# A written order of all steps in place of one computed from ranks, in a DeltaNet and low-rank mixer kernel

## The chip, the cores and the metric

One NeuronCore of a Trainium2 chip runs the whole kernel. It has five engines with instruction streams of their own: TensorE (PE: matmuls, PEld: its weight loads), VectorE (DVE), ScalarE (ACT), GpSimd (POOL) and SyncE (SP, which here only issues DMAs). [...] The metric is the device time of one launch in microseconds; a lower time is better. A time is the median of several runs.

## The reference

A DeltaNet attention for 4 batches, 8 heads, 768 tokens and 48 channels, whose output `x` goes through a low-rank token mixer and a two-layer channel mixer:

```python
k_n = k / (np.linalg.norm(k, axis=-1, keepdims=True) + 1e-06)
for t in range(S):
    y[:, :, t] = np.einsum('bhd,bhde->bhe', q[:, :, t], state)
    v_old = np.einsum('bhde,bhd->bhe', state, kt)
    state = state + bt[:, :, :, None] * np.einsum('bhd,bhe->bhde', kt, vt - v_old)
x = y.transpose(0, 2, 1, 3).reshape(B, S, H * D)
h = x.transpose(0, 2, 1) @ U @ V
u = x + h.transpose(0, 2, 1)
return u + np.maximum(u @ w_ch1, 0.0) @ w_ch2
```

## The kernel before

**Work.** Tokens are cut into chunks of 64 (12 to a batch, `c`). Half a batch (6 chunks, all heads) is a unit `n`, eight in all; unit 2b and 2b+1 belong to batch `b`. Two large tiles, `slots`, hold the operands of an even and an odd unit, so that unit n+2 overwrites unit n. Of a unit the kernel makes, in this order:

- `load` (L531): DMAs of k, q, v and a second copy z of k, on SyncE's and GpSimd's queues, 4 heads each.
- `grams`: `turn` (L633) transposes k and q by TensorE, `placed` (L648) copies them out by ScalarE, `products` (L661) makes k k^T and k q^T, which ScalarE (L671, L681) and VectorE (L674, L692) copy and mask.
- `blocks` (L737 to L759): VectorE inverts the 32-row triangles by substitution, pairs of L746 and L752, between two transposes; `seed` (L731) clears the tile for it on GpSimd. `norms` (L593 to L610) scales it.
- `joins` (L768 to L869) and `diagonals` (L881, L888) put the triangles of 32 together to 64 by small matmuls (L802, L816, L842, L845, L860, L863).
- for units 0 and 1, `prepare` (L961, L972) multiplies the inverse into k and v ahead of the recurrence.

`recur(b)` then goes through the chunks of a batch: a product with the state (L1051 for units 0 and 1, L1010 and L1034 later), a subtraction (L1064 or L1022), the update's product (L1079) and the state's sum (L1089). `outputs` makes a chunk's y (L925, L939) and `put` copies it into the tile X (L909). Each of these products is 8 matmuls on quarters of TensorE's array.

The weights of the mixers come as 14 slices (`load_weights`): DMA (L1166), and per slice two VectorE steps (L1193, L1199), a ScalarE cast (L1174) and a third VectorE step (L1205) that frees the buffer for the slice after the next. `sums` (L1119) adds slices of the second matrix to one another.

The mixers work on blocks `i` of 256 tokens, three to a batch. `front` makes u and its transpose (L1372 to L1418). `wide` is the channel mixer: `channels` e = 0 to 5 multiplies by two column blocks of the first matrix, in a form of 128 rows (L1475, mode "F") or on quarters of 64 rows (`crossed`, L410, mode "Q", with a one-column copy L419 by ScalarE half way), `relu` (L1440) takes the result from PSUM, `add_up` (L1502) and `last_sum` form sums, `narrow` e = 0 to 3 does the seven products of the second matrix (L1590 or again L410), and `gather` (L1515) adds them into X and sends out a finished block. Batch 3's first layer is done by `quick` (L1275 and around), six strands of seven matmul steps each.

**PSUM.** Four pairs of banks take everything up to the mixers; when all but the last chunk of batch 0 is through, `reserve` takes the fourth pair away, and its two banks, the "mix" banks, belong to `channels`, `narrow` and `quick`.

**Order.** Each of the functions above is a generator. It yields either a list of keys that have to be emitted first (`need`) or a step `op(engine, cost, ...)`; resumed, it writes that step's instructions and goes on to its next yield. The order in which steps are resumed is the order in which instructions stand in the engines' streams; nothing reorders them afterwards, and the semaphores follow from which tiles a step reads and writes. `run` chooses the next step with a clock of its own for each engine: of the steps that can start soonest it takes the one with the lowest rank. The rank of a part is the number in the table `PLACES` under its name (`recur b0 -6.39`, some 600 entries), and an entry `quad 1` allows the part the 64-row form:

```python
at, i = min(picks)                       # earliest start, then lowest rank
cost = cost_of(s)                        # a written estimate of the step's time
state["now"] = clock[s["e"]] = at + cost
advance(i, got, state["now"] + s["lat"])
```

The order so found has 692 steps of TensorE, 720 of VectorE, 501 of ScalarE, 158 of GpSimd and 166 of SyncE.

Of the kernel before, what the change touches and what calls it, by code (L numbers as in the profile page):

```python
# [1 line left out]

# [5 lines left out]

# [8 lines left out]

# [6 lines left out]

QUADS = ((0, 0), (1, 1), (1, 0), (0, 1))


@with_exitstack
def kernel(
    ctx: ExitStack,  # L30
    tc: tile.TileContext,
    q: bass.AP,
    k: bass.AP,
    v: bass.AP,
    beta: bass.AP,
    moe_U: bass.AP,
    moe_V: bass.AP,
    moe_w_ch1: bass.AP,
    moe_w_ch2: bass.AP,
    out: bass.AP,  # L40
):

    nc = tc.nc  # L50

# [16 lines left out]
    W2 = 2 + 2 * KT  # L68

    const = ctx.enter_context(tc.tile_pool(name="const", bufs=1))  # L70
    single = ctx.enter_context(tc.tile_pool(name="single", bufs=1))
    small = ctx.enter_context(tc.tile_pool(name="small", bufs=2))
    conv = ctx.enter_context(tc.tile_pool(name="conv", bufs=2))
    mix = ctx.enter_context(tc.tile_pool(name="mix", bufs=2))
    scratch = ctx.enter_context(
        tc.tile_pool(name="scratch", bufs=2, space=bass.MemoryType.DRAM)
    )
    psum = ctx.enter_context(
        tc.tile_pool(name="psum", bufs=1, space=bass.MemoryType.PSUM)
    )  # L80

    P = psum.tile([128, 8, 512], FP32, name="P")
    BANK = dict(pair=[0, 2, 4, 6], mix=[6, 7])

    clock = dict(port=0.0, pe=0.8, dve=0.8, act=0.8, pool=0.8, sp=0.8)
    state = dict(now=0.0, mode=None, hw=0.0, slow=1.9, lot=69, fetched=0.0, flow=0.0, span=0)
    free = dict(pair={x: 0.0 for x in range(4)}, mix={})
    done, parts, waits, ready, last = {}, {}, {}, {}, {}  # L90
    asked, missing, awaited, woken, quads = {}, {}, {}, [], set()
    LAT = dict(pe=0.22, dve=0.06, act=0.06, pool=0.1, sp=0.0)
    SWITCH, HOLD, STAY = 0.18, 0.18, 0.15
    LOT, FETCH = 256, 4.1
    SPAN, PHASE = 3.413, 2.0

    def dve(n):
        return (n + 151) / 1000.0

    def act(n):  # L100
        return 0.16 + n / 1200.0

    def op(
        engine, cost, mode=None, take=None, give=(), lat=None, rush=None, words=0, port=None, flow=None,
        after=(),
    ):
        return dict(
            after=after,
            flow=cost * 0.95 if flow is None else flow,
            e=engine, cost=cost, mode=mode, take=take, give=give, words=words + 0.4,  # L110
            port=engine == "pool" if port is None else port,
            rush=bool(give) if rush is None else rush, lat=LAT[engine] if lat is None else lat,
        )
# [4 lines left out]
    def emitted(key, after=0.0):  # L118
        done[key] = state["now"] + after
        for i in awaited.pop(key, ()):  # L120
            missing[i].discard(key)
            if not missing[i]:
                woken.append(i)

    def landing(packets, each=0.0205):
        state["hw"] = max(state["hw"], state["now"] + 1.0) + packets * each / 16
        return state["hw"] + 0.4 - state["now"]

    def advance(i, value, at):
        try:  # L130
            s, ready[i] = parts[i].send(value), at
        except StopIteration:
            waits.pop(i, None)
            return
        if isinstance(s, list):
            waits.pop(i, None)
            asked[i], missing[i] = s, {key for key in s if key not in done}
            for key in missing[i]:
                awaited.setdefault(key, []).append(i)
            if not missing[i]:  # L140
                woken.append(i)
        else:
            waits[i] = s

    PLACES = """
    add_up b0 i0 17.5; add_up b0 i1 115.48; add_up b0 i2 71; add_up b1 i1 10.76; add_up b1 i2 15.15
    add_up b2 i0 54.56; add_up b2 i1 63.94; add_up b2 i2 115.5; add_up b3 i0 -4.22; add_up b3 i1 62.29
    add_up b3 i2 42; blocks n1 40.91; blocks n2 26.26; blocks n3 92.86; blocks n4 49.5; blocks n5 78.95
    blocks n6 36.67; blocks n7 136.31; both -6; channels b0 i0 e1 24.46; channels b0 i0 e2 52.34
    channels b0 i0 e3 47.17; channels b0 i0 e4 51.28; channels b0 i0 e5 -8.66; channels b0 i1 e0 52.04  # L150
    channels b0 i1 e0 quad 1; channels b0 i1 e1 79.42; channels b0 i1 e2 120.05; channels b0 i1 e3 96.5
    channels b0 i1 e3 quad 1; channels b0 i1 e4 13.79; channels b0 i1 e5 26.76; channels b0 i2 e0 quad 1
    channels b0 i2 e1 88.32; channels b0 i2 e1 quad 1; channels b0 i2 e2 92.17; channels b0 i2 e2 quad 1
    channels b0 i2 e3 128.97; channels b0 i2 e4 12; channels b0 i2 e4 quad 1; channels b0 i2 e5 88
    channels b0 i2 e5 quad 1; channels b1 i0 e0 40.95; channels b1 i0 e0 quad 1; channels b1 i0 e1 59
    channels b1 i0 e1 quad 1; channels b1 i0 e2 96.8; channels b1 i0 e2 quad 1; channels b1 i0 e4 91
    channels b1 i0 e4 quad 1; channels b1 i0 e5 69.5; channels b1 i0 e5 quad 1; channels b1 i1 e1 123.7
    channels b1 i1 e1 quad 1; channels b1 i1 e2 47.06; channels b1 i1 e2 quad 1; channels b1 i1 e3 -2.83
    channels b1 i1 e4 -16.29; channels b1 i1 e4 quad 1; channels b1 i1 e5 99.12; channels b1 i1 e5 quad 1
    channels b1 i2 e0 62.73; channels b1 i2 e0 quad 1; channels b1 i2 e2 35.08; channels b1 i2 e3 93.63  # L160
    channels b1 i2 e3 quad 1; channels b1 i2 e4 -29.18; channels b1 i2 e5 10.16; channels b1 i2 e5 quad 1
    channels b2 i0 e0 107; channels b2 i0 e1 41.61; channels b2 i0 e2 12.5; channels b2 i0 e2 quad 1
    channels b2 i0 e3 100.05; channels b2 i0 e3 quad 1; channels b2 i0 e4 17.5; channels b2 i0 e5 68.5
    channels b2 i1 e0 -1.5; channels b2 i1 e0 quad 1; channels b2 i1 e1 107.29; channels b2 i1 e1 quad 1
    channels b2 i1 e2 -7.68; channels b2 i1 e2 quad 1; channels b2 i1 e3 -3.95; channels b2 i1 e4 33.5
    channels b2 i1 e4 quad 1; channels b2 i2 e0 0.4; channels b2 i2 e0 quad 1; channels b2 i2 e1 22.31
    channels b2 i2 e1 quad 1; channels b2 i2 e2 21.63; channels b2 i2 e2 quad 1; channels b2 i2 e3 7.38
    channels b2 i2 e3 quad 1; channels b2 i2 e4 90.57; channels b2 i2 e5 quad 1; copies 0; cut 9
    diagonals n0 h0 -0.5; diagonals n0 h1 107.22; diagonals n1 h0 48.5; diagonals n1 h1 -9.5; diagonals n2 h0 12
    diagonals n2 h1 67.42; diagonals n4 h0 15; diagonals n4 h1 22.77; diagonals n5 h0 66.26; diagonals n5 h1 66.6  # L170
    diagonals n6 h0 49.61; diagonals n6 h1 75; diagonals n7 h0 65.5; diagonals n7 h1 71.44; first 71.59
    first_of_last 8.76; front b0 i0 46.95; front b0 i0 quad 1; front b0 i1 41.01; front b0 i2 58.06
    front b1 i0 30.2; front b1 i1 45.12; front b1 i2 142.26; front b1 i2 quad 1; front b2 i0 46.76
    front b2 i0 quad 1; front b2 i1 6.48; front b2 i1 quad 1; front b2 i2 66.34; front b3 i0 56.8
    front b3 i1 110.5; front b3 i2 18.13; gather b0 i0 h0 c1 70.62; gather b0 i0 h1 c0 116.5
    gather b0 i0 h1 c1 103.04; gather b0 i1 h0 c0 57.42; gather b0 i1 h0 c1 47.56; gather b0 i1 h1 c0 101.5
    gather b0 i1 h1 c1 114; gather b0 i2 h0 c0 78.4; gather b0 i2 h1 c0 54.71; gather b0 i2 h1 c1 59.36
    gather b1 i0 h0 c0 60.5; gather b1 i0 h0 c1 110; gather b1 i0 h1 c1 16.38; gather b1 i1 h0 c0 7
    gather b1 i1 h0 c1 0.46; gather b1 i2 h0 c0 81; gather b1 i2 h0 c1 76; gather b1 i2 h1 c0 93.52
    gather b1 i2 h1 c1 -12; gather b2 i0 h0 c0 67; gather b2 i0 h0 c1 29.97; gather b2 i0 h1 c0 26.5  # L180
    gather b2 i0 h1 c1 46.69; gather b2 i1 h0 c0 12.5; gather b2 i1 h0 c1 4; gather b2 i1 h1 c1 -0.93
# [76 lines left out]
    wide b0 i2 113.63; wide b1 i0 110.97; wide b1 i1 12; wide b1 i2 100.81; wide b2 i1 94; wide b2 i2 81.54  # L258
    wide b3 i1 10; wide b3 i2 -7.5
    """  # L260
    PLACES = dict(x.strip().rsplit(" ", 1) for x in PLACES.replace("\n", ";").split(";") if x.strip())

    def name_of(part):

# [42 lines left out]
    def late(s, at):  # L307

        over = state["lot"] + s["words"] - LOT
        if s["e"] != "pe" or over <= 0:  # L310
            return 0.0, 0.0
# [1357 lines left out]
```

## Time and profile before

| what | value |
|---|---|
| three runs | 611.9, 611.78, 609.16 us; median 611.78 |
| profiled execution, span | 609.6 us (its own time is not given apart from the span) |
| instructions in the profile | 24754 |
| costliest group | L1475, `channels` in 128-row form: 420 records, 97.2 us |
| second | L1590, `narrow`: 456 and 240 records, 79.5 and 41.6 us |
| third | L410, 64-row form: 912 records, 62.5 us |
| chain that ended last | PE 71%, DVE 8%, ACT 2%, issue 2% of the span |
| HBM | 27.03 MB read, 4.72 MB written |

A matmul in 32-bit floats leaves two records, so 12 records of L1475 are 6 matmuls. The span is the time from the first to the last instruction. A group of the profile is known by the source line that issued it and the tiles it writes and reads (`P<-ut,w_sb` writes PSUM from the transposed u and the first matrix). `<-ACT hs L1440` behind an idle time names what ended it; "issue" is idle time that ended without anything the profile shows. TensorE's granted clock is given as a share of its full speed.

### The profile page before, as it was taken

The numbers are of one execution on the slowest core, as the hardware profiler recorded it, in microseconds if no ns is written. First come the engines' busy times: TensorE is split into PE (matmuls) and PEld (weight loads), VectorE is DVE, ScalarE is ACT, GpSimd is POOL, SyncE is SP. The second block draws the span as 40 slices with busy tenths as digits, with TensorE's granted clock in tenths as the row PEclk, the third lists the DMA queues.
The fourth block names the chain that finished last, engine by engine and source line by source line (L and its number), as shares of the span: only waits on it lengthen the run. The fifth ranks groups of instructions, "written<-read, shape, count | busy, mean of one in ns | idle before, by whom it ended". The sixth has DMA issues, their size and how long they took to land.

```text
span 609.6 us, 24754 instructions
## 1 busy us (share of the span) xinstructions
PE 569.9 (93%) x11178; PEld 480.4 (79%) x11178; DVE 395.1 (65%) x972; ACT 235.9 (39%) x498; POOL 97.7 (16%) x169
## 2 busy tenths in 40 slices
PE   4797776999999998999999899999999999999997
PEld 4697765788889787888879767988888768656997
DVE  5889966798893232899899428998993225332542
ACT  3566863634242343344332633244225321344000
POOL 8321124420010126003005230020001000000000
PEclk9656575899999999999999999999999999999999
DMA  9951759610000156101006133020000000000000
GB/s 142 165 149 52 252 173 166 120 41 4 28 3 6 44 81 117 49 2 41 29 3 100 49 74 49 16 53 3 30 2 3 30 3 1 26 1 1 19 34 26
DMA packets 63849, 33.34 MB, mean 55 GB/s; under 512 B 50816, under 2 KB 61824, under 8 KB 63744
## 3 DMA queue, kind: packets, MB, share of 16 engines
q1 hardware_dynamic: 56800, 23.21, 17.7%
q0 software_dynamic: 5344, 8.27, 6.5%
q8 instruction: 87, 1.43, 1.0%
q10 hardware_dynamic: 1600, 0.30, 0.3%
q14 instruction: 18, 0.15, 0.1%
HBM read 27.03 MB, written 4.72 MB: 52 GB/s over the span
## 4 chain that ended last, share of the span: by engine, by line
PE 71%; DVE 8%; ACT 2%; issue 2%; DVEq 0%; ACTq 0%
PE P L1590 22%; PE P L1475 13%; PE P L410 12%; PE P L1275 7%; PE P L633 2%; PE P L661 2%; DVE xt L752 2%; DVE prod L746 2%; PE P L1034 2%; PE P L1010 1%; PE P L925 1%; PE P L1079 1%; ACT hs L1440 1%; PE P L1372 1%; PE P L939 1%
## 5 line engine op out<-in xcount | busy, mean ns | idle before, releaser
L1475 PE MATMUL P<-ut,w_sb 128*128 128x256 f32 x420 | 97.2, 384 | 0.2
L1475 PEld LDWEIGHTS P<-ut,w_sb 128*128 128x128 f32 x420 | 77.8, 190 | 11.2 <-ACT hs L1440 0.9
L1590 PE MATMUL P<-w_sb,hs 128*128 128x192 f32 x456 | 79.5, 329 | 0.0
L1590 PEld LDWEIGHTS P<-w_sb,hs 128*128 128x128 f32 x456 | 74.0, 190 | 2.8 <-ACT hs L1440 0.9
L1515 DVE TENSOR_TENSOR X<-X,P 128x192 f32<-128x192 f32 x85 | 29.6, 352 | 62.7 <-PE P L1590 55.1
L752 DVE TENSOR_TENSOR xt<-xt,prod 128x112 f32<-128x112 f32 (+21 forms) x200 | 64.6, 323 | 6.9
L746 DVE TENSOR_TENSOR prod<-gs,xt 128x112 f32<-128x112 f32 (+21 forms) x200 | 64.1, 321 | 4.9
L410 PE MATMUL P<-ut,w_sb 64*64 64x256 f32 x912 | 62.5, 384 | 1.2 <-ACT hs L1440 0.2
L1440 ACT ACTIVATE hs<-P 128x512 f32<-128x512 f32 x54 | 32.3, 597 | 74.0 <-PE P L1475 56.1
L531 POOL DMA_DIRECT2D slot<-in_k_dram x44 | 28.9, 664 | 95.4 <-PE P L1079 94.5
L1590 PE MATMUL P<-w_sb,S 128*128 128x192 f32 x240 | 41.6, 328 | 0.0
L633 PE MATMUL P<-ident,slot 128*128 128x128 f32 x192 | 31.6, 317 | 8.6 <-DMA slot<-in_k_dram 7.0
L909 ACT COPY X<-P 64x192 f32<-64x192 f32 x96 | 30.0, 312 | 24.0 <-PE P L939 22.0
L1590 PEld LDWEIGHTS P<-w_sb,S 128*128 128x128 f32 x240 | 39.0, 190 | 0.2
L410 PEld LDWEIGHTS P<-ut,w_sb 64*64 64x64 f32 x912 | 29.7, 133 | 10.5 <-ACT hs L1440 1.7
L648 ACT COPY slot<-P 128x768 f32<-128x768 f32 x30 | 23.5, 801 | 36.1 <-PE P L633 35.9
L1089 DVE TENSOR_TENSOR s<-s,P 128x192 f32<-128x192 f32 x40 | 14.0, 351 | 33.0 <-PE P L1079 30.2
L633 PEld LDWEIGHTS P<-ident,slot 128*128 128x128 f32 x192 | 25.8, 163 | 11.7 <-issue 9.7
L1275 PE MATMUL P<-slot,w_sb 128*128 128x384 f32 x96 | 34.6, 492 | 0.1
L881 ACT COPY slot<-zz 32x384 f32<-32x384 f32 x64 | 32.3, 509 | 6.1 <-DVE zz L759 4.7
L661 PEld LDWEIGHTS P<-slot 48*64 48x64 f32 x1536 | 29.3, 150 | 6.5 <-issue 2.8
L661 PE MATMUL P<-slot 48*64 48x64 f32 x1536 | 31.9, 237 | 0.6 <-ACT slot L648 0.5
(157 smaller groups left out, 966.1 us busy)
## 6 DMA issues: line engine op xcount, KB each, us to landing
out_dram<-X SPq DMA_DIRECT2D x22, 192.0 KB, 1.9
X<-in_moe_w_ch_dram SPq DMA_DIRECT2D x10, 384.0 KB, 4.2
wide<-in_moe_w_ch_dram SPq DMA_DIRECT2D x10, 384.0 KB, 4.5
slot<-in_k_dram SPq DMA_DIRECT2D x48, 72.0 KB, 5.0
slot<-in_k_dram POOLq DMA_DIRECT2D x44, 72.0 KB, 5.1
slot<-in_q_dram POOLq DMA_DIRECT2D x32, 72.0 KB, 5.0
slot<-in_q_dram SPq DMA_DIRECT2D x32, 72.0 KB, 5.0
slot<-in_v_dram POOLq DMA_DIRECT2D x32, 72.0 KB, 3.0
```

What stands on the lines that cost most here:

```text
L410: nc.tensor.matmul(to[half(g)], w[half(r), half(g)], x[half(r)], start=start, stop=stop, skip_group_check=True,)
L633: nc.tensor.transpose(p_t[:, c // 3, c % 3], t[:, c, 2 * j : 2 * j + 2].rearrange("p s d -> p (s d)"), ident,)
L661: nc.tensor.matmul(p_g[half(g ^ (par * i)), par, c], kq[rows, c, j, 0, half(g)], kq[rows, c, j, i, half(g)], start=True, stop=True,)
L746: nc.vector.tensor_tensor(out=prod, in0=gb[:, :, j : j + 1, j + 1 :].to_broadcast([128, split, m, w]), in1=xb[:, :, 0:m, j : j + 1].to_bro ...
L752: nc.vector.tensor_tensor(out=xb[:, :, 0:m, j + 1 :], in0=xb[:, :, 0:m, j + 1 :], in1=prod, op=ALU.subtract,)
L881: nc.scalar.copy(pg[quarter(i), :, at, :, a : a + BK], cut(zc, h)[quarter(i)].rearrange("p r (c j) t -> p r c j t", j=2),)
L909: nc.scalar.copy(x[half(c % 2), c // 2, 4 * D * g : 4 * D * (g + 1)].rearrange("p (j r d) -> p r j d", r=2, d=D), states(p_y)[half(g)],)
L1275: nc.tensor.matmul(to, w, t, start=start, stop=stop, skip_group_check=True)
L1440: nc.scalar.activation(hs[:, fs[0] : fs[1] + 1 : fs[1] - fs[0]], p_f, ACTF.Relu)
L1475: nc.tensor.matmul(p_f[:, x], w(x, t), ut[:, t], start=(t == 0), stop=(t == KT - 1))
L1515: nc.vector.tensor_tensor(out=to, in0=to, in1=p, op=ALU.add)
L1590: nc.tensor.matmul(to, of[0], of[1], start=of[2], stop=of[3], skip_group_check=True)
```

## The change

The planner goes: `PLACES`, the ranks, the engines' clocks, the costs in `op`, the bookkeeping of banks and the choice between the two forms. In its place stands a string `ORDER` of 2228 tokens. A token is the number of a part (parts are numbered as they begin); `38` resumes part 38, `14.0` resumes part 14 and gives it pair of banks 0, `269q` resumes part 269 in the 64-row form where both are offered. The order was found by exchanges of single steps.

```diff
-    def run():
-        stall, forms = {}, {}
-        while waits or woken:
...
+    ORDER = """
+    1 0 1 0 1 0 1 0 1 38 22 38 22 21 22 14.0 36 22 21 2 151 36 43 15.1 151 38 37 36 37 152 153.2 21 43 152 36
...
+    def run():
+        wake()
+        for token in ORDER.split():
+            i, bank, quad = (token.partition('q')[0] + '.').split('.')[0], token.partition('.')[2], 'q' in token
+            step = waits[int(i)]
+            if isinstance(step, tuple):
+                step = step[quad]
+            mode[0] = step['mode'] or mode[0]
+            fixed = step['take'][1] if isinstance(step['take'], tuple) else None
+            first = fixed[0] if isinstance(fixed, tuple) else fixed
+            advance(int(i), int(bank) if bank else first)
+            wake()
+        assert not waits and not awaited
```

Four waits that the clocks had implied are written into the generators' lists: a unit counts as read only when the outputs of its last three chunks are written; `relu` waits for weight slice 7, whose landing buffer is the tile it writes; a block of batch 3 waits for the sum of the block before. The last `channels` of a block is offered in the 128-row form alone:

```diff
             if cu == UC - 1:
-                emitted(("rec", n), 0.5)
+                yield [('y', b, c - 1), ('y', b, c - 2)]
+                emitted(('rec', n))
...
-        yield need(("front", b, i), ("half" if b == LAST else "narrow", *before(b, i), *[3] * (b == LAST)))
+        yield need(('front', b, i), *([('half', *before(b, i), 3), ('summed', *before(b, i), 6)] if b == LAST else [('narrow', *before(b, i))]))
...
         def relu(fs, ms, p_f):
-            yield op("act", act(2 * GT), give=[("mix", m) for m in ms])
+            yield [('weights', 7)]
+            yield op('act')
...
-            yield (
-                op("pe", 1.3, "F", take=("mix", y % 2), words=12),
-                op("pe", 0.87, "Q", take=("mix", (0, 1)), words=32),
-            )
-            if parted():
+            plain = op('pe', mode='F', take=('mix', y % 2))
+            last = y == len(PAIRS) - 1
+            yield (plain if last else (plain, op('pe', mode='Q', take=('mix', (0, 1)))))
+            if parted() and (not last):
```

The steps themselves, their tiles, buffers and queues are the same. The new order has 686 steps of TensorE (5658 matmuls for 5712: three `channels` with e = 5 change their form), 720 of VectorE, 498 of ScalarE, 158 of GpSimd and 166 of SyncE. Of TensorE's steps 389 stand in the same sequence as before, of VectorE's 408, of ScalarE's 268; a TensorE step that both orders have is moved by 4.9 places on average (at most 46), a VectorE step by 8.7 (at most 69).

## The prediction

> **What bounds the kernel now.** I read the page's busy times first, then the busy time by stage, then the chain of waits, and last the order of VectorE's instructions where the chain leaves TensorE.
>
> ```profile
> PE 569.9 (93%) x11178; PEld 480.4 (79%) x11178; DVE 395.1 (65%) x972; ACT 235.9 (39%) x498; POOL 97.7 (16%) x169
> ```
> ```profile
> PE   4797776999999998999999899999999999999997
> PEclk9656575899999999999999999999999999999999
> ```
> ```profile
> 0.00:111.00 111.00, 84.53 (x2436) 76.67 (x2440) 85.77 (x208) 64.01 (x121) 39.26 (x71) 0.65 0.74 158
> 111.00:606.00 495.00, 485.01 (x8758) 403.76 (x8746) 308.99 (x763) 171.86 (x378) 58.48 (x99) 1.00 0.15 32
> 606.00:610.00 4.00, 0.32 (x2) 0.02 (x1) 0.35 (x1) 0.00 (x0) 0.00 (x0) 0.83 0.08 25
> ```
>
> TensorE sets the end, in two unlike stages. In the second table each row is a stage: its length, then busy us of PE, PEld, DVE, ACT, POOL, then the granted clock. Up to 111 us (loads, the triangular solves, batch 0's recurrence) TensorE is idle for 111.0 - 84.5 = 26.5 us and runs at a mean clock of 0.65, VectorE being busy for 85.8 us: a chain through three engines bounds it. From 111 to 606 us TensorE is idle for 10 us and the clock is 1.00. The last 4 us are the final add and store.
>
> Busy time hides short waits, since a pipelined group that starts late still counts as busy. So I took each group of matmuls (one step of the order) from its start to the start of the next, and as its undisturbed time the 20th percentile of the same kind after 112 us. From 112 us to the end the groups take 42.8 us more than undisturbed, of some 498: that is what an order could at most give back there. 14.8 us of it stand at 102 changes of the matmul tiling (128, 64 or 32 rows), 0.145 us each. Four stretches of 1.29 to 1.72 us, 6.0 together, wait for nothing that the profile shows ("issue"). Most of the rest is short waits like these, on the chain of waits (start, us, what):
>
> ```profile
> 302.47 0.61 ACT hs L1440
> 303.12 1.09 PE P L410 x16
> 305.28 0.97 PE P L410 x16
> 307.28 0.60 ACT hs L1440
> 307.93 1.09 PE P L410 x16
> ```
>
> The chain leaves TensorE twice in 6 us for the 0.60 us activation that frees the two mix banks: only two groups of 0.41 us stand between the matmuls it reads and those that want the banks.
>
> **The change, part by part.** *The planner and its costs* run while the program is built: no instruction, 0 us. *The four added waits* are lists that hold a step back until other steps are written; no instruction, 0 us, whatever they forbid is already in the written order. *Three `channels` of e = 5* go from 64-row to 128-row form: 24 small matmuls become 6 large ones (54 fewer matmuls in all) and three L419 copies go (0.16 us each, on ScalarE, 39% busy). Both forms have the same array work: 6 records of L1475 take 1.29 us and 24 of L410 some 1.3 us, two of each to a channel; taken as 0, between -0.5 us (three copies that TensorE no longer waits for) and +0.9 us (six entries at 0.145). *Tiling changes* go from 129 to 131: 2 x 0.145 = +0.3 us.
>
> *The order after 112 us.* 337 groups of the old order there wait for a ScalarE or VectorE instruction. I call a cover short when the matmul time that stands between the group which that instruction waited for and the group which waits for it is less than the instruction's own time (with up to six queued ahead of it) plus 0.35 us of handing over; in the rows above an L1440 starts 0.25 us or so after its last matmul's group and the L410 behind it 0.05 us after its end, its weight load having waited 0.26. Old order: 54 short covers, new order: 25 of 329. In the trace a group with a short cover is late by 0.284 us on average (tiling changes left aside), another by 0.034. By number: 29 x 0.25 = 7.2 us gained. By name: 44 short covers go, with 9.7 us of lateness in the trace apart from tiling changes, less 1.7 of an "issue" stretch and 38 x 0.034 that stays: -6.7; 15 come, now 2.5 us late, 15 x 0.284 = 4.3 then: +1.8; net -4.9. I take -6.0, between the two. Example: for `channels` b1 i1 e1 of the rows above the new order puts the two halves of e0 side by side and three small groups (1.2 us) behind them.
>
> *VectorE beside it.* The substitutions of units 4 and 5 are drawn forward. Over 80 us of undisturbed matmul time from batch 0's second token block on, the new order holds 89.8 us of VectorE work; the old order's densest 80 us held 84.6, and the pace of the trace (498 for 455) gives such a stretch 87.5. Bounds: 0, if overlapping starts cover it as they do from 280 to 320 us (36.1 busy of 40), and +3.3, if VectorE decides and the gain there is lost with it. I take +1.5.
>
> *The start.* The recurrence of batch 0 stands on two waits for weight slices:
>
> ```profile
> 91.94 0.35 DVE L1064 TENSOR_TENSOR z<-slot,P 128x192 f32<-128x192 f32 x1 [1.22 <-PE P L1051]
> 94.17 0.56 DVE L1193 TENSOR_SCALAR power<-X 128x768 int32<-128x768 int32 x1 [1.87 <-DMA X<-in_moe_w_ch_dram]
> 94.64 0.74 DVE L1199 TENSOR_SCALAR X<-X 128x768 int32<-128x768 int32 x1
> 95.31 0.34 DVE L1089 TENSOR_TENSOR s<-s,P 128x192 f32<-128x192 f32 x1
> ...
> 99.72 0.56 DVE L1193 TENSOR_SCALAR power<-wide 128x768 int32<-128x768 int32 x1 [1.59 <-DMA wide<-in_moe_w_ch_dram]
> 100.20 0.35 DVE L1064 TENSOR_TENSOR z<-slot,P 128x192 f32<-128x192 f32 x1
> ```
>
> L1193 opens a weight slice. It waits 1.87 and 1.59 us for its DMA, and the recurrence's L1089 and L1064 are queued behind it, TensorE behind those (2.4 and 1.4 us). The new order writes the first of the two after the next chunk's update and the second two chunks later. The same 7.5 us of weight work stays among these chunks. Against that, slice 13 is asked for later too: its buffer is freed by a conversion that now comes two steps later, and on SyncE's queue the loads of unit 2 stand ahead of slices 12 and 13 (SP's issues take some 0.65 us each; this slice took 9.2 us from issue to use). So between 0 and 3.5 us are gained here. Earlier, batch 0's chunks 2 to 5 come forward by 5 to 8 us of matmul and VectorE work, but what unit 1's half needs (`prepare`, L961) has 4.0 us more of TensorE's and 3.5 us more of VectorE's work ahead of it, and four of its groups have covers short by 1.5 to 2 us behind ScalarE's queue: between 0 and +4. At `front` of batch 0 the work ahead is equal again on TensorE, VectorE and ScalarE. POOL's and SP's first loads are interleaved among each other with the same number of issues; 0. Start in all: I take -2.0, between -3.5 and +4.
>
> **Sum**: -6.0 + 1.5 - 2.0 + 0.3 = -6.2 us. The profiled execution has a span of 609.6; its own time is not shown, and the runs (609.2 to 611.9) put it within 2.3 us of the span. From the median: 611.8 - 6.2 = 605.6, say **605.5 us**.
>
> [...] The four "issue" stretches lie where small matmuls are dense (1.5 us before an L860), and the instruction queue moved 87 packets, 1.43 MB. [...]
>
> **The rivals.**
> 1. *More than that*: the start gives its whole 3.5 us and the "issue" stretches fall on other, slower groups (-4): 611.8 - 7.2 - 3.5 - 4 + 0.3 = 597. For it: they are few and depend on where a dense run meets a load. Against: the dense runs are still there. 0.13.
> 2. *VectorE becomes the bound* where units 4 and 5 are solved: the full 3.3 us, and of the 6.0 the third that lies there is lost: 611.8 - 4 + 3.3 - 1 = 610. For it: 84.6 to 89.8 us. Against: 65% over the span, and 5.8 us of work in the 20 us before. 0.13.
> 3. *Slower: unit 1 comes late.* If chunk 6 of batch 0 has to wait for `prepare` of unit 1, the start ends 4 us later by the queues ahead of it, and as TensorE has the full clock only from 110 us on, some 4 us of the mixer's first matmuls fall into half clock and cost 4 more: 611.8 + 8 - 4.5 = 615. It decides from the point at which `prepare` is later than the chunk before it, which in the old trace had some 4 us to spare (83.1 against 86.8 us). 0.13.
> 4. *The order does nothing*: the waits that go are replaced by the next one behind, as when a bank is held by two readers; 611 to 612. 0.09.
>
> [...]
>
> **How the numbers follow.** My forecast has 0.52. Range 597 to 613: it takes in rivals 1 and 2 and my own case (600 to 609), and leaves out most of rival 3. Within 0.5% (3 us) is no change that this measurement can tell: up to 608.7 is faster. Faster: 0.48 of my case, 0.13, 0.03 of rival 2: 0.64. Slower: 0.11 of rival 3 and a few hundredths: 0.14. Same: 0.22.
>
> **What would show it.** Right: from 112 us on fewer L1440 and L1089 on the chain, the rows "PE <- ACT hs L1440" and "PEld <- ACT hs L1440" smaller; between 111 and 606 us (or its counterpart) 4 to 6 us less; no DMA ahead of L1193's counterpart in batch 0's recurrence; the full clock from some 108 us. Wrong: DVE at 95% or more for 80 us with PE waiting for `rest` or `s`; the first `front` later than 111.5 us; "issue" stretches of more than 6 us.

## The result, and the profile after

The new order is slower: 620.1 us (median of 4 runs, 619.3 to 620.5) against 611.84 (4 runs, 609.2 to 613.4) beside it; the ratio is 1.013, 95% interval 1.0096 to 1.0164. The profiled execution after has a span of 617.6 us against 609.6, 8.0 us more.

Busy times, and TensorE with its clock in 40 slices, from the page of the kernel after:

```profile
PE 570.7 (92%) x11070; PEld 485.2 (79%) x11070; DVE 389.4 (63%) x972; ACT 232.2 (38%) x495; POOL 97.5 (16%) x169
```
```profile
PE   3768886899999999999999999999999999999997
PEclk9975655599999999999999999999999999999999
```

The stages of the kernel after, with the columns of the table in the prediction:

```profile
0.00:122.00 122.00, 88.36 (x2424) 81.20 (x2428) 85.12 (x208) 63.62 (x120) 37.17 (x68) 0.68 0.63 140
122.00:614.00 492.00, 482.00 (x8658) 404.00 (x8650) 303.88 (x763) 168.55 (x375) 60.31 (x102) 1.00 0.16 33
614.00:618.00 4.00, 0.30 (x2) 0.00 (x1) 0.35 (x1) 0.00 (x0) 0.00 (x0) 0.86 0.08 25
```

The busy times hardly moved, so work was not added; it stands at other times. The mixer's stage got shorter, 492 us where it took 495. The start got longer: TensorE is idle in it for 122.0 - 88.4 = 33.6 us, against 26.5. Measured at one point, the first group of the first `front` (batch 0), the start ends at 122.6 us in place of 111.5 (+11.2, with the decimals that the table leaves out), and what follows takes 495.0 in place of 498.2 (-3.2).

Where TensorE waits in the whole kernel after (line, what for, us in total, times, longest):

```profile
PE P L375 <- DMA slot<-in_k_dram: 6.9, 2, 5.4
PE P L324 <- DMA X<-in_beta_dram: 6.0, 1, 6.0
PE P L503 <- DVE power L777: 4.0, 1, 4.0
PE P L690 <- ACT w_sb L763: 3.4, 1, 3.4
PE P L1102 <- DVE X L1048: 2.1, 4, 1.0
```

The first row is the wait for the first keys, which the old order has too. The second is new. L324 is the transposition of beta (L562 before). The chain of waits goes through it (start, us, what), after:

```profile
11.61 7.42 DMA X<-in_beta_dram
19.03 0.04 issue
19.07 1.46 PE P L324 x22
20.53 1.49 PE P L375 x6
22.04 0.81 ACT slot L386
```

And the same transposition on TensorE's timeline, first after, then before:

```profile
19.07 1.46 PE L324 MATMUL P<-ident,X 16*64 16x16 f32 x22 [6.04 <-DMA X<-in_beta_dram]
```
```profile
14.04 0.93 PE L562 MATMUL P<-ident,X 16*64 16x16 f32 x24
```

`load_beta` brings beta in two transfers on POOL's queue. The old order writes them side by side. The new one writes seven loads of units 0 and 1 and a memset between them. POOL's timeline, first before, then after:

```profile
5.54 1.21 POOL L551 DMA_DIRECT2D X<-in_beta_dram  x2
6.74 4.00 POOL L531 DMA_DIRECT2D slot<-in_k_dram  x6
```
```profile
5.57 0.62 POOL L313 DMA_DIRECT2D X<-in_beta_dram  x1
6.18 2.62 POOL L301 DMA_DIRECT2D slot<-in_k_dram  x4
8.77 0.68 POOL L301 DMA_DIRECT2D slot<-in_q_dram  x1
9.41 0.69 POOL L301 DMA_DIRECT2D slot<-in_k_dram  x1
10.05 1.03 POOL L445 MEMSET xt<- 128x1056 f32 x1
10.97 0.69 POOL L301 DMA_DIRECT2D slot<-in_q_dram  x1
11.61 0.62 POOL L313 DMA_DIRECT2D X<-in_beta_dram  x1
```

So POOL issues the second transfer at 11.61 us instead of 6.15, and it lands 7.4 us after its issue, at 19.0. In TensorE's stream the transposition stands ahead of the other work, and TensorE is idle for the 6 us until then. By the steps of the order, traced in both kernels (start in us):

| step | before | after | later by |
|---|---|---|---|
| first step of unit 0's substitution (L741, after L454) | 17.3 | 25.1 | 7.8 |
| the transposition that ends it (L759, after L464) | 26.7 | 38.5 | 11.8 |
| first step of unit 1's substitution | 44.8 | 51.7 | 6.9 |
| `prepare` of unit 1, second group | 80.8 | 93.7 | 12.9 |
| `recur` of batch 0, step 26 | 91.2 | 101.9 | 10.7 |
| first `front` | 111.5 | 122.6 | 11.2 |
| last `narrow` | 604.2 | 612.2 | 8.0 |

### The profile page after: what moved, and what is told of

It is laid out like the page before. It is cut to its first block, busy times and chain, and to the rows that moved or that the text cites. A ratio compares the mean times of both kernels' runs of the same rounds, so it can differ in the third digit from the quotient of the medians.

```text
span 617.6 us, 24523 instructions
## 1 busy us (share of the span) xinstructions
PE 570.7 (92%) x11070; PEld 485.2 (79%) x11070; DVE 389.4 (63%) x972; ACT 232.2 (38%) x495; POOL 97.5 (16%) x169
## 3 DMA queue, kind: packets, MB, share of 16 engines
q8 instruction: 87, 1.43, 1.0%
## 4 chain that ended last, share of the span: by engine, by line
PE 64%; DVE 25%; issue 3%; DMA 3%; ACT 2%; POOL 2%; DVEq 0%; SPq 0%; ACTq 0%; POOLq 0%
PE P L1102 19%; PE P L1014 10%; PE P L201 8%; PE P L838 7%; DVE xt L460 5%; DVE prod L459 5%; PE P L375 3%; PE P L398 3%; DVE gs L450 2%; PE P L515 2%; PE P L503 2%; DVE zz L464 1%; PE P L604 1%; PE P L597 1%; PE P L662 1%
## 5 line engine op out<-in xcount | busy, mean ns | idle before, releaser
L1014 PE MATMUL P<-ut,w_sb 128*128 128x256 f32 x456 | 106.7, 385 | 0.2
L1014 PEld LDWEIGHTS P<-ut,w_sb 128*128 128x128 f32 x456 | 83.9, 190 | 13.4 <-issue 1.8
L1102 PE MATMUL P<-w_sb,hs 128*128 128x192 f32 x456 | 79.7, 329 | 1.0 <-DVE X L1048 1.0
L1102 PEld LDWEIGHTS P<-w_sb,hs 128*128 128x128 f32 x456 | 73.9, 190 | 2.7 <-DVE X L1048 1.3
L1048 DVE TENSOR_TENSOR X<-X,P 128x192 f32<-128x192 f32 x85 | 29.5, 350 | 57.6 <-PE P L1102 54.2
L201 PE MATMUL P<-ut,w_sb 64*64 64x256 f32 x768 | 52.3, 384 | 1.8 <-ACT hs L984 1.2
L1102 PE MATMUL P<-w_sb,S 128*128 128x192 f32 x240 | 41.2, 328 | 0.4 <-DVE X L1048 0.3
L1102 PEld LDWEIGHTS P<-w_sb,S 128*128 128x128 f32 x240 | 39.0, 190 | 1.3 <-DVE X L1048 1.2
L301 POOL DMA_DIRECT2D slot<-in_k_dram x44 | 29.2, 668 | 63.3 <-PE P L604 33.6
L386 ACT COPY slot<-P 128x768 f32<-128x768 f32 x30 | 23.7, 800 | 34.1 <-PE P L375 33.9
L398 PE MATMUL P<-slot 48*64 48x64 f32 x1536 | 33.5, 244 | 2.0 <-ACT slot L386 2.0
L838 PE MATMUL P<-slot,w_sb 128*128 128x384 f32 x96 | 33.2, 486 | 0.0
L201 PEld LDWEIGHTS P<-ut,w_sb 64*64 64x64 f32 x768 | 25.4, 133 | 9.4 <-ACT hs L984 2.5
```

The costliest lines, as they stand in the source:

```text
L201: nc.tensor.matmul(to[half(g)], w[half(r), half(g)], x[half(r)], start=start, stop=stop, skip_group_check=True)
L398: nc.tensor.matmul(p_g[half(g ^ par * i), par, c], kq[rows, c, j, 0, half(g)], kq[rows, c, j, i, half(g)], start=True, stop=True)
L838: nc.tensor.matmul(to, w, t, start=start, stop=stop, skip_group_check=True)
L1014: nc.tensor.matmul(p_f[:, x], w(x, t), ut[:, t], start=t == 0, stop=t == KT - 1)
L1048: nc.vector.tensor_tensor(out=to, in0=to, in1=p, op=ALU.add)
L1102: nc.tensor.matmul(to, of[0], of[1], start=of[2], stop=of[3], skip_group_check=True)
```

## The experiments

All kernels are the kernel after with another ORDER, or with a few of its steps moved; e3, e4 and e7 also take back one of the added waits, and e8 offers one more `channels` call in the 64-row form. "Rest" is the time from the first `front` to the start of the last `narrow`, from the profile. The runs e1 to e7 and e9 ask where the start's loss is, e8 and e10 to e12 what the order of the mixer is worth.

| run | what it is | time, us | ratio to before, 95% | first front | rest |
|---|---|---|---|---|---|
| before | | 611.5 to 612.6 | | 111.5 | 492.7 |
| after | | 620.1 | 1.0096 to 1.0164 | 122.6 | 489.5 |
| e1_beta | beta's second transfer early | 611.9 | 0.9979 to 1.0018 | 116.2 | 489.4 |
| e2_oldstart | old start, new rest | 610.7 | 0.9957 to 0.9999 | 112.2 | 489.7 |
| e3_newstart | new start, old rest | 623.7 | 1.0157 to 1.0217 | 123.2 | 495.5 |
| e4_oldlate | old order in the new form | 613.9 | 1.0011 to 1.0054 | 113.1 | 493.0 |
| e5_earlyold | e1, first half of the start old | 610.3 | 0.9963 to 1.0002 | 114.4 | 489.1 |
| e6_lateold | e1, second half of the start old | 612.9 | 0.9983 to 1.0028 | 116.2 | 490.3 |
| e7_oldlate2 | old order, second transfer late | 617.8 | 1.0069 to 1.0134 | 116.8 | 492.6 |
| e8_quad | e2, four channel calls in 64-row form | 614.5 | 1.0017 to 1.0066 | 112.8 | 493.1 |
| e9_subst | e1, first substitution undisturbed | 611.5 | 0.9982 to 1.0024 | 114.6 | 489.8 |
| e10_covers | e1, 46 more short covers | 628.8 | 1.0241 to 1.0333 | 115.5 | 505.4 |
| e11_best | e2, four exchanges | 611.6 | 0.9977 to 1.0025 | 113.4 | 490.7 |
| e12_changes | e1, 70 more changes of tiling | 622.2 | 1.0129 to 1.0202 | 117.4 | 499.7 |

**One step moved.** Part 2 is `load_beta` of the first half; its second token goes up by 31 places.

```diff
-22 21 2 151 36 43 15.1
+22 21 2 2 151 36 43 15.1
...
-25 19 2 39 2
+25 19 39 2
```

> The new order with one single step moved: the second of the two transfers of beta on POOL's queue stands right behind the first again, ahead of seven loads of units 0 and 1. Theory A (the late half of beta is the loss): the first substitution step starts near 18 us instead of 25.1, TensorE's wait of 6.0 us for beta shrinks under 1 us, the first front comes 7 us sooner (115 to 116 us), and the time falls from 620.1 to 612-614. Rival B (the weight slices ahead of VectorE's and ScalarE's work set the end of the start): whatever is gained at the first substitution is waited away before the first front; 618 or more. Rival C (what lies after the first front lost as well): irrelevant to this kernel's difference, it stays above the kernel before in both cases.

611.9 us: 8.2 less than after, and level with the kernel before. TensorE's wait for beta is gone. Its timeline in this run (this kernel's lines stand 5 lower):

```profile
12.46 1.46 PE L319 MATMUL P<-ident,X 16*64 16x16 f32 x24
```

The first substitution starts at 18.5 us, 6.6 earlier, and the later steps of the table, up to the last `narrow`, are 6.1 to 6.6 us earlier than after. So nothing downstream absorbs the wait, and rival B is out.

**Old start with new rest, new start with old rest.** The cut is the first group of the first `front`; ahead of it stand nearly the same steps in both orders.

```diff
-(steps ahead of `front` b0 i0, new order)
+(the same steps, old order)
...
```

> All steps up to the first front in the old order, everything after it in the new one. If the loss is in the start alone and the two parts add up: first front at 111.5 us as before, then the 495.0 us that the new order took from there, a span of 606.5 and a time of 608.7 (3 us under the kernel before). Rival: the gain after the first front exists only because a late start had already done its VectorE work; then this kernel takes 611-613. If the new order loses after the front what the trace hides: over 613.

> All steps up to the first front in the new order, everything after it in the old one. If the parts add up: first front at 122.6 us, then the 498.1 us of the kernel before, a span of 620.7 and a time of 623. Rival (the rest gains only by the late start): 620 or less.

610.7 and 623.7. The start is worth 9.4 us (620.1 - 610.7) and the new rest 3.0 us in the trace (489.7 against 492.7), nearly alike whichever start it follows: 489.1 to 490.3 us in the six runs that have it unchanged. Old rest behind the new start took 495.5. The parts add up to within 2 us; the sum expected for the first of the two was 608.7. Some of that is the spread of the old start: with the same order of TensorE's, VectorE's and ScalarE's steps up to there the first `front` came at 111.5, 112.2, 112.8, 113.1 and 113.4 us in five executions (before, e2, e8, e4, e11).

**Beta late in the old order.** The first try moved the second token of `load_beta` behind eight other steps of POOL, but that part has a third step, which issues nothing, and so the transfer stayed where it was. What ran is the old order in the new form, with three `channels` of e = 5 in 128-row form (and a wait on `outputs` of batch 3 taken back, which the old order doesn't meet).

```diff
-2 2 2
+2 2
...
+2
```

> The old order with one step moved: the second transfer of beta behind the loads of k and z of unit 1 (eight steps on POOL's queue), about where the new order has it. Theory A: the first substitution starts 6 to 8 us late and the time rises from 611.8 to 617-620. Rival B: under 614, since the old order has slack elsewhere in its start.

613.9 us, 2.0 more than the kernel before by the ratio, and the control for the next run, which moves two tokens and with them the transfer.

```diff
-2 2 2
+2
...
+2 2
```

> The old order with the second transfer of beta really moved behind eight other steps of POOL's queue (the earlier run of this name moved a step that issues nothing, and so shows the old order in the new form). Theory A (the place on the queue is the loss): TensorE's wait for beta grows to 4-7 us, the first substitution step starts at 23-25 us in place of 18.2, time 4 to 8 us over that earlier run: 618-622. Rival (only the new order suffers, for it has beta's matmuls ahead of other work on TensorE): the first substitution starts under 20 us, time under 616.

617.8 us, 3.9 over its control and just under what theory A expected. The wait is there:

```profile
19.27 1.46 PE L324 MATMUL P<-ident,X 16*64 16x16 f32 x22 [4.47 <-DMA X<-in_beta_dram]
```

The first substitution starts at 22.5 us in place of 18.2. The same late transfer thus costs 4 us in the old order and 8 in the new. From the end of the wait to that step it takes 3.2 us here (22.5 - 19.3) and 6.0 after (25.1 - 19.1). What differs is ScalarE's queue: after, the square root of the norms (L344), which the substitution needs as well, is queued behind the copy L386, and L386 behind a turn on TensorE that stands behind beta:

```profile
22.04 0.80 ACT L386 COPY slot<-P 128x768 f32<-128x768 f32 x1 [0.47 <-PE P L375]
22.74 0.26 ACT L344 ACTIVATE norm<-gs 128x32 f32<-128x32 f32 x1
```

L344 ends at 23.0 us, and VectorE's next instruction for the norms starts at 23.03. This second part was read from the trace and not tried alone.

**What is left of the start.** With beta early the first `front` is still at 116.2 us (115.5 and 117.4 in two other executions of the same start, e10 and e12), some 4 us later than with the old start; e1 comes out level with the kernel before because its rest is shorter by 3. Two halves of the start, divided at the first step of unit 1's substitution, were put back by turns, and then the first substitution alone.

```diff
-(blocks n0, with other groups' steps of VectorE in between)
+(blocks n0, steps 1 to 16 one after the other, as in the old order)
...
```

> The new order with its first stretch alone (up to the first step of unit 1's substitution, both transfers of beta early) put back into the old order; from there to the end the new order. The run with only beta moved left the first front at 116.2 us, against 111.5 to 113.1 in the runs of the old start. Theory A2 (what is left comes from VectorE's steps of unit 0 and 1 put between the steps of the first substitution, which take 13.4 us in place of 9.4): the first front comes at 112-113 us, time 608-609. Theory C (what is left comes later, from unit 1's joins written behind the recurrence's chunks 2 to 5): first front at 115 to 116.5, time 611-612.5.

> The converse: the new first stretch with beta's second transfer early, then the old order from the first step of unit 1's substitution to the first front, then the new order. Theory C: first front at 112 to 113.5 us, prepare of unit 1 at 83 us or so in place of 87.7, time 608.5-610.5. Theory A2: first front at 115 to 116.5, time 611-612.5.

> The new order with beta early, and of the start only the stretch from the first step of unit 0's substitution to the first of unit 1's in the old order: the loads stay in the new order, and VectorE runs the 16 steps of the first substitution without the eight other steps in between. Theory A2 (those eight steps are what is left of the loss): the substitution takes 9.4 us in place of 13.4, time 610 to 610.8 against 611.9 with beta early alone. Rival (the order of the first loads is what is left): 611.5 to 612.5.

The first half gives 1.6 us by the medians (610.3 against 611.9), which the intervals do not tell from nothing, and the second gives nothing (612.9), so theory C is out: unit 1's `prepare` came at 84.2 us in that run, as expected, and the first `front` still at 116.2. The first substitution alone gives 1.6 us in the trace (114.6) and 0.4 in the runs (611.5, where its rival expected 611.5 to 612.5). What stretches it can be read in the run with only beta moved:

```profile
24.78 0.29 DVE L455 TENSOR_TENSOR xt<-xt,prod 128x126 f32<-128x126 f32 x1
26.50 0.56 DVE L412 TENSOR_TENSOR slot<-P,mask_u 128x384 f32<-128x384 f32 x1 [1.43 <-PE P L393]
26.98 0.28 DVE L454 TENSOR_TENSOR prod<-gs,xt 128x128 f32<-128x128 f32 x1
```

Two instructions of the substitution, L455 and L454, that need nothing but VectorE are 2.2 us apart, since a product written between them waits 1.43 us for its matmuls. Five such steps stand in the stretch (the expectations counted eight), which takes 13.3 us in place of 9.4. How much of what is left belongs to this and how much to the order of the first loads or to the second half stays open: runs of one kernel differ by 3 to 5 us, and the medians here by 1.6 or less.

**Covers.** In 42 places after the first `front` a group of matmuls that waits for ScalarE or VectorE changes places with the group ahead of it, on TensorE alone and within one tiling.

```diff
-outputs b3 c4 / channels b2 i1 e1
+channels b2 i1 e1 / outputs b3 c4
...
```

> Beta early (611.9), and after the first front 42 pairs of neighbouring groups of matmuls exchanged on TensorE alone, all within one tiling, so that the group that waits for ScalarE or VectorE stands one place nearer to the group it depends on: by the same count as in the prediction 71 short covers in place of 25, the changes of tiling stay 109. Theory (a short cover costs 0.284 us, another group 0.034): 46 x 0.25 = 11.5 us more, 623 us. Rival (the next group's wait is shortened by what this one waits, so that pairs of waits cost as one; most of them lie inside the recurrences' chains): 3 us more or less, 615.

628.8 us, 16.9 over the same kernel without the exchanges, more than expected. The mixer's stage of this run, and of the run with beta early that it is made from:

```profile
115.50:622.50 507.00, 486.29 (x8615) 402.63 (x8609) 304.78 (x763) 167.53 (x374) 60.46 (x102) 1.00 0.15 32
```
```profile
115.50:607.50 492.00, 482.19 (x8650) 403.95 (x8642) 303.96 (x763) 168.39 (x375) 60.12 (x102) 1.00 0.15 33
```

VectorE, ScalarE and the clock have the same work; TensorE is idle for 20.7 us in place of 9.8, and shows 4.1 us more as busy. By groups (start to start, against the undisturbed time of the kind) those with a short cover are late by 17 to 20 us more in sum than without the exchanges, and the others by 2 to 4 us less; the ranges come from tighter and looser bounds for a short cover. The rest as a whole is 16.0 us longer, so 46 more short covers cost 0.35 each on balance.

**Changes of tiling.** First four channel calls that the new order runs in 128-row form, between 64-row groups, were brought into 64-row form.

```diff
-recur b1/34, e3/0 (F), recur b1/36
+e3/0 (Q), recur b1/34, e3/1 (Q), ScalarE's copy, recur b1/36
...
```

> The old order up to the first front, the new one after it, and there four channel calls that the new order runs in the 128-row form as islands between 64-row groups (b0 i2 e3, e4, e5 and b1 i2 e4) in the 64-row form: 12 changes of the matmul tiling fewer, four more copies of 0.16 us on ScalarE each pair of banks, 96 small matmuls for 24 large ones less. Theory (a change of tiling costs 0.15 to 0.18 us whatever the order, and the mixer's gain was partly paid with six more of them): 1.8 to 2.1 us less than the same kernel without this, which had 610.7: 608.5 to 609. Rival (the islands are worth their changes, as they let one bank be read while the other is written; in the 64-row form both banks are held and the covers get short): no gain or a loss, 610.5 to 613.

614.5 us: a loss of 3.8, where a gain of 2 was expected; around the three calls of b0 i2 the trace loses 2.4 us. In 64-row form a call holds both mix banks and has a copy (0.16 us) in its middle, and in 128-row form it holds one of them and leaves the other to `relu`. That this is where the loss comes from is read from the kernel; the saved changes in any case don't pay for it. So this run can't price a change, and another was made that leaves the covers nearly as they are: 35 pairs of groups exchanged at the border of two tilings.

```diff
-channels b0 i0 e4/1 (F) / joins n2 h0/4 (J)
+joins n2 h0/4 (J) / channels b0 i0 e4/1 (F)
...
```

> Beta early (611.9), and after the first front 35 pairs of neighbouring groups exchanged at the border between two tilings, where no cover gets short by it (27 short covers in place of 25): 179 changes of the matmul tiling in place of 109. Theory (a change of tiling costs what the groups at changes were late by in the traces, 0.145 us in the old order's and 0.177 in the new order's, whatever waits there): 70 x 0.145 to 0.177 = 10 to 12.4 us, and 0.5 to 0.7 for two covers, 622.5 to 625. Rival (the lateness at changes is that of waits that happen to stand there, the change itself costs next to nothing): under 615.

622.2 us, 10.3 over the kernel that it was made from, for 70 changes: 0.147 each, 0.14 when two short covers that came with it are taken off; the intervals of the two runs allow 0.11 to 0.18. The mixer's stage:

```profile
117.50:619.00 501.50, 491.90 (x8612) 404.11 (x8610) 304.25 (x763) 167.37 (x374) 60.01 (x102) 1.00 0.15 32
```

Its idle time is 9.6 us, the same as without the changes (9.8). All of the cost stands in TensorE's busy time, 491.9 in place of 482.2. A view of waits can't show it.

So a change of the tiling cost 0.14 to 0.15 us here; what passes inside TensorE this run does not show.

**A try at a better version.** Old start, new rest and four exchanges that the prices above would favour:

```diff
-recur b2/66, outputs b2 c10/1
+outputs b2 c10/1, recur b2/66
...
```

> The old order up to the first front, the new one after it (610.7), with four exchanges of neighbouring groups there that shorten no cover and lengthen one: 24 short covers in place of 25, 108 changes of tiling in place of 109. By the prices above 0.25 + 0.17 us less: 610.3, which can't be told from 610.7, and 1 to 1.5 us less than the kernel before. If it is over 611.5, the earlier gain of the old start with the new rest was chance.

611.6 us, where the kernel before took 612.6 beside it and the ratio is 1.0001. That is over the 611.5 above which, as was set beforehand, the earlier gain would be chance. In each of the three kernels with the old first half of the start and the new rest (e2, e5, e11) the median is 1.0 to 1.2 us under that of the kernel before, but their intervals reach to 0.9999, 1.0002 and 1.0025: clearly faster than the kernel after, and not shown to be faster than the one before.

## Why the prediction was wrong

It forecast 605.5 us (597 to 613, slower with a chance of 0.14), and 620.1 came. The term of the start failed. For the mixer's stage the sum had -6.0 + 1.5 + 0.3 = -4.2, and -3.2 came, which is near in part by luck: the gain from covers was smaller, and stretches that the sum left as they were became shorter.

The latenesses below are sums over the groups behind the first `front`, counted as in the prediction. How many covers are short depends on where the bound is drawn; with a bound that marks 55 groups before and 35 after, the parts are: short covers -4.1, "issue" stretches -3.0, changes of tiling +1.7, all other groups +2.8, the three `channels` in their other form -0.5.

- **The start, -2.0 (between -3.5 and +4); +11.2 in the trace.** The step that failed is "POOL's and SP's first loads are interleaved among each other with the same number of issues; 0". I counted the issues on a queue and didn't ask which load is wanted first: the second half of beta went back by seven loads and a memset. Moved forward alone it gives 8.2 us of the 8.3 by the runs, and 6.5 of the 11.2 in the trace. What was argued there at length, the recurrence's waits for weight slices (-3.5 to 0) and `prepare` of unit 1 (0 to +4), does not explain the loss: TensorE waits 3.4 us behind a weight slice after (L690 for L763, a slice whose DMA takes 5.8 us), where it waited 2.4 and 1.4 before, and `prepare` put back to its old time gained nothing (e6). The other 4 us or so of the start stay open; up to 1.6 of them may lie in its first half.
- **Short covers, -6.0; -4.1.** Right in mechanism, by e10, and a third smaller than forecast. In the traces the groups with a short cover are late by 13.7 us in sum before and 9.6 after, "issue" stretches left aside; looser bounds, up to 119 and 91 short groups, give -4.6 to -5.6. The price of 0.284 us that I used stood for the covers that these orders leave short, by little; where e10 shortens them further, they cost 0.35 each on balance.
- **Changes of tiling, +0.3; +1.1 to +1.7.** The price was right (0.145 against 0.147 and 0.14 in e12). The number was not: 129 to 131 counts the start too, where other things set the end. After the first `front` it is 103 to 109, and the groups there are late by 15.7 us in place of 14.6, or by 14.2 in place of 12.5 without those that have a short cover as well. Six changes at 0.147 make 0.9 of it; the rest I take for waits that stand at changes.
- **VectorE's dense stretch, +1.5; some +2.** Behind the first `front` TensorE waits for VectorE for 4.3 us in sum, in place of 2.0, and at most for 1.0 at once, in place of 0.4. The densest 80 us found in the trace after (from 250 us) hold 75.8 us of VectorE, and from 256 to 302 us the chain of waits runs over VectorE almost alone; it ends in the longest of these waits (L1102 for L1048). The chain's shares of the span after, and its end there (start, us, what):

```profile
PE 64%; DVE 25%; issue 3%; DMA 3%; ACT 2%; POOL 2%; DVEq 0%; SPq 0%; ACTq 0%; POOLq 0%
```
```profile
301.46 0.41 DVE prod L459
301.89 0.40 DVE xt L460
302.29 0.27 DVE X L1048
302.57 0.04 issue
302.61 2.22 PE P L1102 x12
```

  VectorE had 8% of the chain before. So it sets the pace of the new order in places, which the bounds of 0 and +3.3 allowed for.
- **Three `channels` in 128-row form, 0 (-0.5 to +0.9).** In the old order they are hardly free: the control e4 takes 2.0 us more than the kernel before (0.7 to 3.3 by the interval). Its trace shows 8 changes of tiling more, 103 to 111, and two calls at which it loses 1.4 and 1.1 us, but a rest that is only 0.2 us longer in all, since its "issue" stretches are 2.1 us shorter; so the size isn't settled. In the new order the 128-row form is the better one for the four calls of e8.
- **The rivals.** The slower one (unit 1 late, 615 us) had the right sign and the wrong place. Its condition was nearly met (with beta early the chunk named there starts 1.2 us behind the second group of `prepare`, 88.9 and 87.7, where it had 6.0 us before), but the old order of the stretch in question, e6, gained nothing. Its second price, matmuls that fall into half clock, has no counterpart: TensorE's clock goes from 0.50 to 1.00 at 110.3 us before and at 121.9 us after, in both just ahead of the first `front` (111.5 and 122.6), and its mean is 1.00 from 111 to 606 us before and from 122 to 614 us after. That mixer matmuls behind a late start fall into half clock was my estimate, and no run shows it; nor is 110 us the first time at full clock, since it is 1.00 from 80 to 85 us before as well. The order was no idle change either, as the mixer's 3 us show.
- **The "issue" stretches.** The sum left their 6.0 us in, and 3.0 us went. Behind the first `front` the kernel before has four in which TensorE is idle for more than 0.25 us, 3.7 us together, and the kernel after two, 1.2 us together; with the groups around them they make 4.7 (where the prediction had 6.0) and 1.7 us of lateness. Two of them, before:

```profile
237.61 2.01 PE L410 MATMUL P<-w_sb,S 64*64 64x192 f32 x43 [0.95 <-issue]
242.49 0.27 PE L1034 MATMUL P<-rest,slot 64*64 64x48 f32 x3 [0.93 <-issue]
```

  Counted along TensorE's stream in the trace (matmuls, weight loads, waits), these two lie 255 instructions apart, and all six such stretches in the traces before and after stand at the same place of every 256 instructions, to within one. The instruction queue brought 87 packets of 16 KB in the span of each (1.43 MB), and the traces have 88 such places before and 87 after. With one packet to each place but the first, in order, no place is passed sooner than 1.27 us after its packet's landing before and 1.40 us after, and the six waits ended 1.40 to 1.60 us after it. That TensorE waits there for this packet is my reading of these numbers; no run varied it. Of the 88 places before, four behind the first `front` show more than 0.25 us. That the stretches depend on where a dense run meets a load, as the first rival has it, no run shows.

## What to carry to other kernels

When an order is rewritten, write down for each engine the first load that it will wait for and what stands ahead of that load on its queue, in both orders: one transfer of 48 KB, put behind seven others, cost 8.2 us where the new order of the mixer brought 3. Test a start and the rest as hybrids of the two orders, since one such run says which half lost and one moved step says why. A list of waits did not price the changes of tiling here, whose 9.7 us (e12) stand in busy time; exchanges of neighbours that leave the covers nearly as they are did. And the place of a stretch in which TensorE waits for nothing visible can be counted: here all six stood at one place of every 256 instructions, and they ended 1.40 to 1.60 us after a packet of the instruction queue had landed.

## What was not expected of the hardware

- A change of the matmul tiling cost 0.14 to 0.15 us (0.11 to 0.18 by the intervals) of TensorE time that the profile shows as busy: in e12, 70 of them raised the busy time of the mixer's stage by 9.7 us (482.2 to 491.9) and the idle time not at all (9.8 and 9.6).
- A transfer of 48 KB took 5.5 us from issue to landing when it was issued at 5.6 us and 7.4 us when it was issued at 11.6 us, behind seven loads of 72 KB on its queue: it is later by 1.9 us more than its place.
- The start of the same order is not fixed: up to the first `front` the old order took 111.5 to 113.4 us in five executions, and the new one with beta early 115.5 to 117.4 in three, while the new order's rest repeats within 1.2 us (489.1 to 490.3) behind six different starts.
- TensorE's waits without a visible cause of more than 0.25 us behind the first `front` (four before, two after) all stand at one place of every 256 of its instructions, to within one, and ended 1.40 to 1.60 us after a 16 KB packet of the instruction queue had landed.
